# One unit fewer inside the second scan of a complex recurrence followed by a mixture of experts

## The chip, the cores and the metric

The kernel runs on one core of one Trainium2 chip. The metric is the device time of one execution in microseconds (us); the times shown are those of separate executions, and the profile is of one more execution.

## What is computed

A complex diagonal recurrence over 768 steps for 4 batches and 8 heads of 48 channels, and then a mixture of 8 experts (of which each token takes one) on its 3072 output rows. Cut to what matters:

```python
for t in range(S):                                   # S = 768
    new_re = ar * S_re - ai * S_im                   # ar, ai: a_re, a_im with their magnitude capped
    new_im = ar * S_im + ai * S_re
    kv = einsum('bhd,bhe->bhde', k[:, :, t], v[:, :, t])
    S_re, S_im = new_re + kv, new_im
    y[:, :, t] = einsum('bhd,bhde->bhe', q[:, :, t], S_re)
x = y as 3072 rows of 384
expert = argmax(x @ w_gate);  gate = softmax(x @ w_gate)[expert]
out[i] = gate[i] * (relu(x[i] @ w1[expert[i]]) @ w2[expert[i]])
```

## The kernel before

**Attention, in chunks.** The 768 steps are cut into 8 chunks of 96. Within a chunk the recurrence is turned into products: `Att.scan_ops` runs backwards over the 96 steps on VectorE (DVE) and builds the running products of the complex coefficients, 128 rows (batch, head, chunk) at a time. There are two groups of 128 rows, g = 0 for batches 0 and 1 and g = 1 for batches 2 and 3, so there is a first scan and a second scan, each in 7 segments of 8 or 16 steps. One step is a multiplication (L221, `xy`) and an addition (L232, `a`), each dependent on the one before. A step is written in one piece each when some other operation stands behind it in the list, and in two halves each where nothing does (`halves`, L234). `norm_ops` prepares the coefficients of a segment, `post_ops` scales q and k by the products (`qko`) and writes them to the DRAM scratch `scr` from POOL (L296, L299).

**Units.** A unit is one chunk of one batch: unit n is chunk n // 2 of batch n % 2, and units 16 and up are those of the second group. A unit loads its rows from `scr` (`qkc`, stage L, on SP), transposes them on TensorE (PE; `tr`, stages T0 to T3, copied out by ScalarE, ACT), multiplies (`pa`, A0 and A1), masks on DVE (M0 and M1, L366), sums the state (S on PE, `s` L375; D on DVE, L385 and L387; U; ZA, L403; ZB, L408; with `sx`, a copy with its halves swapped, by two DMAs), and makes the output (`y`) and the routing. A chunk that is the last of its batch (units 14 and 15) has no S. The table `SLOT` spreads the stages of a unit over several slots: slot n holds S of unit n, T1, T2, T3 and T0 of unit n + 1, the load L of unit n + 2, and so on. In the names printed below, `s_6` is S or D of chunk 6 (unit 12 at its first occurrence, unit 13 at its second), and `tr_7_0_1` is T1 of chunk 7.

**What sets the order.** Units of the first group need only the first scan, so their slots are laid into the second scan, where DVE is the engine with the chain. `Att.dve_ops` writes that order: it gives slot n a due time `t0 + (n + 2) * dt` against a planned length of the scan segments, and places the stages between the steps. Slots that are not placed in the scan or among the operations behind its last step (the `tail`) come in the loop of `tile_recurrence__then__moe_kernel` (L1319), one after another, with nothing of a scan between them. DVE, PE, ACT and SP follow this written order there, and each engine takes its instructions in order.

**The experts.** `Moe.run` loops over 8 experts and 8 slices of 128 hidden columns: `first` (`ph`, L981), ReLU and its rounding rest (`hh`, `hl`), `second` (`my`, L989). Weights come as `raw` and are split in two parts (`hi` by ACT, `lo` by DVE). The rows of the next expert are loaded from `disp` (`xr`, L910, on SP) and turned on PE (`mt`, L919). In this stage the order on PE, DVE and ACT isn't written by hand: a scheduler that plans with estimated times sets it when the kernel is built. SP's order is written.

The lines that the prediction's steps touch are L221, L232, L366, L375, L403, L408 (scan and units), L346 (load of `qkc`), L296 and L299 (`scr`), L870 (weights), L910 and L919 (rows of the next expert).

Of the kernel before, what the change touches and what calls it, by code (L numbers as in the profile page):

```python
# [36 lines left out]
NORM_AT[NS + 4] = NORM_AT[NS + 4][:6] + (.42, .45) + NORM_AT[NS + 4][8:]  # L37
POST_AT = [(0, .138, .138, 0, .42, .421, .55, .55, .68)] * NS + \
          [(.015, .354, .354, .18, .58, .647, .7, .7, .8)] * NS
POST_AT[NS - 2] = (0, .138, .138, 0, .48, .56, .62, .62, .72)  # L40
POST_AT[NS - 1] = (0, .041, .042, .021, .39, .39, .45, .5, .54)

# [7 lines left out]
SLOT_B = [y for x in SLOT_B for y in ([("W", -3)] if x[0] == "R2" else []) + [x] + ([("P", -3)] if x[0] in ("R3", "U") else [])]  # L50

ALONE = 14
CAP = 0.9990000128746033


# [6 lines left out]
class Att:  # L62
# [387 lines left out]
    def dve_ops(self, slots, t0, dt):  # L450


        sl = [(g, j) for g in range(2) for j in range(NS)]
        norms = [self.norm_ops(*x) for x in sl]
        posts = [self.post_ops(*x) for x in sl]
        ahead = [f for x, f in zip(NORM_AT[1], norms[1][1]) if x < 0]
        out = [norms[0][0], norms[1][0]] + norms[0][1][:5] + ahead[:1] + norms[0][1][5:] + ahead[1:]
        now = None
        self.begin = len(out)
        for k, (g, j) in enumerate(sl):  # L460
            if (g, j) == (1, 0):
                now = 0
                self.half = len(out)
            scan = self.scan_ops(g, j)
            at = [(0.13 if k + 1 < len(sl) else .62, 0, posts[k][0])]
            if k + 2 < len(sl):
                at.append((0.16, 0, norms[k + 2][0]))
            if k + 1 < len(sl):
                at += [(x, c, f) for x, c, f in zip(NORM_AT[k + 1], norms[k + 1][2], norms[k + 1][1]) if x >= 0]
            if k + 2 < len(sl):  # L470
                at += [(1 + x, c, f) for x, c, f in zip(NORM_AT[k + 2], norms[k + 2][2], norms[k + 2][1]) if x < 0]
            if k > 0:
                at += zip(POST_AT[k - 1], posts[k - 1][2], posts[k - 1][1])
            if j == 0 and g:
                at.append((0.56, .8, lambda: (self.pend_copy(0), self.pend_test(0), self.pend_cols(0))))
            length = len(scan) * .25 + sum(c for _, c, _ in at)
            if g:
                unit = []

                while slots and slots[0][0] < ALONE and t0 + (slots[0][0] + 2) * dt < now + length:  # L480
                    n, stage, c = slots.pop(0)
                    unit.append((t0 + (n + 2) * dt - now, c, stage))
                    length += c
                at += [(x / length, c, f) for x, c, f in unit]
                now += length

            spots, cur = [[] for _ in scan], 0
            full = [False] * len(scan)
            for x, c, f in sorted(at, key=lambda t: t[0]):
                p = x * len(scan)  # L490
                cur = min(max(p, cur + 1 if c and full[int(cur)] else cur), len(scan) - .01)
                spots[int(cur)].append(f)
                full[int(cur)] |= c > 0
            for i, (op, fs) in enumerate(zip(scan, spots)):
                m = i - i % 2
                out.append(op[not (full[m] and full[m + 1])])
                out += fs

        tail = posts[-1][1]
        out = out[:len(out) - len(spots[-1])]  # L500
        rest = spots[-1]
        while slots[0][0] < ALONE - 1:
            rest.append(slots.pop(0)[1])
        assert len(rest) == 21
        out += tail[:1] + rest[:7] + tail[1:2] + rest[7:11] + tail[2:4] + rest[11:14] + tail[4:] + rest[14:]
        out += [lambda: self.pend_copy(1), lambda: self.pend_test(1), lambda: self.pend_cols(1)]
        return out

# [756 lines left out]
def kernel(ctx, tc, q, k, v, a_re, a_im, w_gate, w1, w2, out):  # L1265
    nc = tc.nc
    const = ctx.enter_context(tc.tile_pool(name="const", bufs=1))
    dram = ctx.enter_context(tc.tile_pool(name="dram", bufs=1, space=DRAM))
    ident = const.tile([128, 128], F32, name="ident")
    flag = const.tile([1, 1], I32, name="flag")  # L1270
    box = {}
    with ExitStack() as c_main, ExitStack() as c_att:
        cp = c_main.enter_context(tc.tile_pool(name="cp", bufs=1))
        x_pool = c_main.enter_context(tc.tile_pool(name="x_pool", bufs=1))
        att = Att(cp, c_att, tc, dram, ident, q, k, v, a_re, a_im)
        disp = dram.tile([E_ * T, XW], F32, name="disp")
        route = att.route = Route(tc, cp, x_pool, att.ps, ident, disp, w_gate, T, CUTS, LATE)
        with ExitStack() as c_moe:
            with ExitStack() as c_dve:
                att.open_dve(c_dve)  # L1280
                hand = {mybir.EngineType.PE, mybir.EngineType.DVE, mybir.EngineType.Activation, mybir.EngineType.SP}
                slots = att.slots()
                ops = att.dve_ops(slots, 6.5, 10.25)
                with tc.manual_schedule(engines={mybir.EngineType.DVE, mybir.EngineType.Activation}):
                    for op in ops[:att.begin]:
                        op()
                with tc.manual_schedule(engines={mybir.EngineType.DVE}):
                    for op in ops[att.begin:81]:
                        op()
                    route.constants()  # L1290
                    clear = route.clear_ops() + att.clear_ops()
                    for i, op in enumerate(ops[81:att.half], 81):
                        op()
                        if i % 8 == 0 and clear:
                            clear.pop(0)()
                    assert not clear
                with tc.manual_schedule(engines=hand):
                    for op in ops[att.half:]:
                        op()
            att.third(c_att)  # L1300
            moe = Moe(c_moe, tc, ident, disp, w1, w2, out)
            with tc.manual_schedule(engines=hand):
                room = [att.bufs["qkc"][i] for i in range(3)]
                route.room = room[:2]
                route.hook, shift, early, end, gates = moe.turn_ops(att.ps, LATE, route.parts, room[2])
                todo = [(14.5, lambda: nc.vector.memset(room[2][C:], 0.0)), (20, moe.numbers)]
                for p in range(Moe.NP):
                    at = 16 + 3 * p
                    todo += [(at, lambda p=p: part(p))]
                todo.sort(key=lambda x: x[0])  # L1310

                def part(p):
                    loads, splits = moe.weight_ops(0, p)
                    loads[0]()
                    n = 16 + 3 * p
                    todo.extend([(n + 1.5, loads[1]), (n + 2.5, splits[0]), (n + 3, splits[1]), (n + 4, splits[2]), (n + 4.5, splits[3])])
                    todo.sort(key=lambda x: x[0])
                loaded = False
                for i, (n, op, _) in enumerate(slots):  # L1319
                    while todo and todo[0][0] <= n:  # L1320
                        todo.pop(0)[1]()
                    op()
                    if n > 30.8 and not loaded:
                        moe.load()
                        loaded = True
                    if i == len(slots) - 9:
                        for kk in range(KT):
                            shift(kk)
                assert not todo and not route.ready
                for kk in range(KT):  # L1330
                    early(kk)
                for kk in range(KT):
                    end(kk)
                route.rest()
                while route.ready:
                    route.pace()
                route.totals()
                gates()
            route.sort()
            moe.order = route.order  # L1340
            covered = uncovered(nc, cp, att.sums, att.small, route, flag)
            c_att.close()
            moe.open(c_moe)
            moe.run(lambda: covered(moe.ps))
    go = nc.values_load(flag, min_val=0, max_val=1)
    with tc.If(go > 0):
        General(tc, dram, ident, q, k, v, a_re, a_im, w_gate, w1, w2, out)
# [27 lines left out]
```

## Time and profile before

| | us |
|---|---|
| the profiled execution | 671.0, its span 669.3 |
| three further executions | 673.67, 674.87, 2745.45 |
| their median | 674.87 |
| mean granted TensorE clock in the profile | 0.92 of full speed |

An engine's busy time is given for stretches of the span, counted in us from its start. Until about 283 us the two scans run; until about 420 us the units of the second group run; then the experts. A row of a timeline gives the start, the duration, the line, the operation, output and inputs, how many instructions were merged, and in brackets the idle time ahead of it with what ended it. An instruction's duration may overlap the next one's: the step from one start to the next start tells what an instruction costs in a stream. The granted clock is 1.00 at 2.4 GHz and 0.50 at 1.2 GHz.

### The profile page before, as it was taken

The page shows a single profiled execution, that of the slowest core. Times are in us where ns is not written, and L with a number is a line of the kernel's source. Part 1 is how long each engine was busy: PE and PEld are TensorE (multiplying, and loading weights), DVE is VectorE, ACT ScalarE, POOL GpSimd, SP SyncE. Part 2 cuts the span into 40 slices and gives each one's busy share as a digit, 9 for nine tenths or more (in the row PEclk, how much of TensorE's full clock was granted, in tenths as well). Part 3 has the DMA queues.
Part 4 walks back from the last instruction along what each step waited for, and adds up shares of the span by engine and source line. Part 5 has one row for each costly group of instructions (what it writes and reads, how often), then busy time and mean ns, then how long its engine had stood idle before and what let it go on. Part 6 is the DMA issues. An engine that isn't in the chain of part 4 may idle for free.

```text
span 669.3 us, 12570 instructions
## 1 busy us (share of the span) xinstructions
PE 544.7 (81%) x4455; PEld 472.1 (71%) x4455; DVE 479.7 (72%) x1428; ACT 345.4 (52%) x789; POOL 92.8 (14%) x140
## 2 busy tenths in 40 slices
PE   0344434248798999899999999999999999999994
PEld 0122212126587877789999888899999999999993
DVE  5999999999999999827657776465455545564531
ACT  7456534476788886544554553244444443443420
POOL 8030000000000000101322221101120202021111
PEclk9776656676899999989999999999999999999998
DMA  5299444596659777776988742583535362636101
GB/s 189 66 319 324 165 165 138 192 224 201 193 163 252 189 180 223 248 152 160 217 228 226 179 111 70 156 252 92 171 94 176 104 182 92 201 88 200 35 35 35
DMA packets 73239, 111.89 MB, mean 167 GB/s; under 512 B 6402, under 2 KB 63045, under 8 KB 71888
## 3 DMA queue, kind: packets, MB, share of 16 engines
q1 hardware_dynamic: 66384, 77.13, 42.7%
q0 software_dynamic: 6784, 33.88, 15.0%
q8 instruction: 37, 0.61, 0.4%
q14 instruction: 34, 0.28, 0.1%
HBM read 72.99 MB, written 34.26 MB: 160 GB/s over the span
## 4 chain that ended last, share of the span: by engine, by line
PE 60%; DVE 23%; ACT 8%; issue 4%; DMA 4%; POOL 1%; SPq 0%; POOLq 0%; DVEq 0%; ACTq 0%
PE ph L981 15%; PE my L989 14%; DVE xy L221 5%; PE tr L354 4%; PE pa L362 4%; DVE a L232 4%; PE s L375 3%; PE y L418 3%; DVE qko L292 2%; PE x L610 2%; PE y L423 2%; DVE a L202 2%; PE xp L135 2%; PE my L1003 2%; PE wp L135 2%
## 5 line engine op out<-in xcount | busy, mean ns | idle before, releaser
L135 PE MATMUL xp<-a,ident 128*128 128x384 f32 x84 | 48.2, 739 | 90.2 <-ACT a L162 90.2
L880 DVE TENSOR_TENSOR lo<-raw,hi 128x384 fp32r<-128x384 f32 (+2 forms) x128 | 66.5, 553 | 65.5 <-ACT hi L879 55.9
L135 PEld LDWEIGHTS xp<-a,ident 128*128 128x128 f32 x84 | 23.0, 289 | 110.1 <-ACT a L162 78.3
L879 ACT CAST hi<-raw 128x384 fp32r<-128x384 f32 (+2 forms) x128 | 60.0, 512 | 55.1 <-PE ph L981 42.5
L221 DVE TENSOR_TENSOR xy<-a 128x96 f32<-128x96 f32 (+1 forms) x299 | 74.6, 279 | 0.6
L354 PE MATMUL tr<-ident,qkc 96*96 96x96 f32 x512 | 65.6, 252 | 11.0 <-DMA qkc<-scr 6.9
L981 PE MATMUL ph<-xh,hi 128*128 128x448 f32 (+4 forms) x192 | 69.7, 365 | 1.1 <-DVE hl L1027 0.9
L981 PE MATMUL ph<-xl,hi 128*128 128x448 f32 (+4 forms) x192 | 67.8, 353 | 0.0
L981 PE MATMUL ph<-xh,lo 128*128 128x448 f32 (+4 forms) x192 | 67.7, 353 | 0.0
L1027 DVE SCALAR_TENSOR_TENSOR hl<-ph,hh 128x448 fp32r<-128x448 f32 (+4 forms) x64 | 37.4, 586 | 39.0 <-ACT hh L1026 37.9
L1026 ACT ACTIVATE hh<-ph 128x448 fp32r<-128x448 f32 (+4 forms) x64 | 32.8, 514 | 61.0 <-PE ph L981 60.6
L989 PE MATMUL my<-hl,hi 128*128 128x448 f32 (+4 forms) x168 | 60.2, 358 | 0.0
L354 PEld LDWEIGHTS tr<-ident,qkc 96*96 96x96 f32 x512 | 47.6, 129 | 17.5 <-issue 6.7
L989 PE MATMUL my<-hh,lo 128*128 128x448 f32 (+4 forms) x168 | 59.9, 356 | 0.0
L989 PE MATMUL my<-hh,hi 128*128 128x448 f32 (+4 forms) x168 | 56.1, 360 | 0.1
L232 DVE TENSOR_TENSOR a<-xy 128x48 f32<-128x48 f32 (+1 forms) x296 | 55.1, 215 | 0.4
L362 PE MATMUL pa<-qT,kT 128*96 128x96 f32 x512 | 54.8, 251 | 0.0
L362 PEld LDWEIGHTS pa<-qT,kT 128*96 128x96 f32 x512 | 50.6, 168 | 1.4 <-issue 1.0
L954 POOL DMA_INDIRECT out_dram<-o,xr x26 | 28.9, 1111 | 157.7 <-DVE o L953 155.9
L630 POOL DMA_INDIRECT disp<-x,idx x32 | 30.1, 939 | 116.5 <-DVE idx L629 64.7
L418 PE MATMUL y<-a_sb,v 128*64 128x96 f32 x512 | 42.3, 253 | 2.3 <-ACT lt L621 1.7
L375 PE MATMUL s<-v,qkc 128*96 128x96 f32 x448 | 44.1, 253 | 0.0
(196 smaller groups left out, 1187.4 us busy)
## 6 DMA issues: line engine op xcount, KB each, us to landing
raw<-in_moe_w_dram SPq DMA_DIRECT2D x64, 384.0 KB
qkc<-scr SPq DMA_DIRECT2D x32, 528.0 KB
scr<-qko POOLq DMA_DIRECT2D x10, 1536.0 KB, 6.9
disp<-fill POOLq DMA_DIRECT2D x7, 772.0 KB, 17.6
v<-in_v_dram SPq DMA_DIRECT2D x32, 144.0 KB
xr<-disp SPq DMA_DIRECT2D x6, 675.5 KB
sx<-s SPq DMA_DIRECT2D x56, 72.0 KB
a<-in_a_re_dram SPq DMA_DIRECT2D x10, 384.0 KB
```

Of the source, the lines that this page charges most:

```text
L135: nc.tensor.matmul(out=pt[:, :m], lhsT=self.ident, rhs=t[:, h:h + m], start=i == 0, stop=i == 1)
L221: nc.vector.tensor_tensor(out=st['xy'][:, :, cs].rearrange("p (u z) d -> p u z d", u=2), in0=crossed(a4[:, s, 1, cs]), in1=w, op=ALU.mult)
L232: nc.vector.tensor_tensor(out=o, in0=xy[:, 0:4:2, cs], in1=xy[:, 1:4:2, cs], op=ALU.add)
L354: nc.tensor.transpose(out=pt[:, h * C:h * C + C], in_=qk(slice(0, C), 4 * hh + h, slice(z_ * C, z_ * C + C)), identity=self.ident[:C, :C])
L362: nc.tensor.matmul(out=pa[:, h * C:h * C + C], lhsT=kT[:, 4 * hh + h], rhs=qT[:, 4 * hh + h], start=True, stop=True)
L375: nc.tensor.matmul(out=ps[:, h * D:h * D + C], lhsT=qk(slice(None), h, slice(C, 2 * C)), rhs=v[:, h * D:h * D + C], start=True, stop=True)
L418: nc.tensor.matmul(out=py[o:o + DP, i // 2 * C:i // 2 * C + C], lhsT=v[:, h * D:h * D + DP], rhs=a_sb[:, h, :], start=True, stop=c == 0)
L879: nc.scalar.copy(out=hi[i][:, s], in_=raw[i][:, s])
L880: nc.vector.tensor_tensor(out=lo[i][:, s], in0=raw[i][:, s], in1=hi[i][:, s].bitcast(F32), op=ALU.subtract)
L981: nc.tensor.matmul(out=ph[:, :WIDTHS[e]], lhsT=a[:, k, fs], rhs=r[:, k, :WIDTHS[e]], start=k == 0 and i == 0, stop=k == KT - 1 and i == 2)
L989: nc.tensor.matmul(out=py[m][:, :WIDTHS[e]], lhsT=a[:, f % self.PF, ms], rhs=r[:, :WIDTHS[e]], start=f == 0 and i == 0, stop=f == NF - 1 a ...
L1027: nc.vector.scalar_tensor_tensor(out=hl[:, :w], in0=ph[:, :w], scalar=0.0, in1=hh[:, :w].bitcast(F32), op0=ALU.max, op1=ALU.subtract)
```

## The change

One table entry, one limit and one spacing change, and the order of three stages behind the scan.

```diff
+POST_AT[-2] = POST_AT[-2][:8] + (.99,)
 ...
 ALONE = 14
+HELD = 13
 ...
-                while slots and slots[0][0] < ALONE and t0 + (slots[0][0] + 2) * dt < now + length:
+                until = HELD if k + 1 < len(sl) else HELD - 2 + 2 / len(SLOT)
+                while slots and slots[0][0] < until and t0 + (slots[0][0] + 2) * dt < now + length:
 ...
-        while slots[0][0] < ALONE - 1:
+        while slots[0][0] < HELD - 1:
             rest.append(slots.pop(0)[1])
 ...
-        out += tail[:1] + rest[:7] + tail[1:2] + rest[7:11] + tail[2:4] + rest[11:14] + tail[4:] + rest[14:]
+        out += tail[:1] + rest[1:3] + rest[:1] + rest[3:7] + tail[1:2] + rest[7:11] + tail[2:4] + rest[11:14] + tail[4:] + rest[14:]
 ...
-                ops = att.dve_ops(slots, 6.5, 10.25)
+                ops = att.dve_ops(slots, 6.5, 10.75)
```

The slots placed in the scan and its tail end one slot earlier (HELD instead of ALONE), the loop of L1319 starts one slot earlier, and the due times of the slots in the scan lie 10.75 instead of 10.25 planned us apart. The last operation of the last but one segment's `post_ops` (which makes `qko` and writes it to `scr`) gets a later place.

On DVE, from the addition that ends the second scan (`pend`), before:

```order
L232 TENSOR_TENSOR pend_131<-xy_6_0_2743 128x2x48
L366 TENSOR_TENSOR a_sb_111<-pa_5_0_2666,mask 96x384
L292 TENSOR_TENSOR qko_5_2600<-a_1_5_1822,v_1_5_2654 128x16x96
L366 TENSOR_TENSOR a_sb_111<-pa_5_1_2707,mask 96x384
L387 TENSOR_TENSOR s_6_2784<-s_6_2746,z_112 96x384
L403 TENSOR_TENSOR sx_5_2662<-sx_5_2662,pcol_98 96x384
```

and at the same place of the changed kernel:

```order
L234 TENSOR_TENSOR pend_131<-xy_6_0_2654 128x2x48
L368 TENSOR_TENSOR a_sb_110<-pa_5_0_2581,mask 96x384
L294 TENSOR_TENSOR qko_5_2512<-a_1_5_1776,v_1_5_2561 128x16x96
L368 TENSOR_TENSOR a_sb_110<-pa_5_1_2628,mask 96x384
L389 TENSOR_TENSOR s_5_2696<-s_5_2658,z_115 96x384
L405 TENSOR_TENSOR sx_5_2577<-sx_5_2577,pcol_98 96x384
```

The stream of units stands one unit further back against the scan: D of unit 12 (`s_6`) stood behind the scan's last step, now D of unit 11 (`s_5`) does. From the second scan's first step to `pend` DVE has 56 operations of units (L366, L385, L387, L403, L408) before and 51 now, and of its 96 steps 35 are written in halves before and 38 now.

On PE, around the two transposes `pt` that read the end of the second scan, before:

```order
L362 MATMUL pa_6_1_2836<-qT_105,kT_108 96x96 x4
L354 MATMUL tr_6_1_1_2843<-ident,qkc_101 96x96 x4
L375 MATMUL s_6_2890<-v_103,qkc_101 96x96 x8
L324 MATMUL pt_0_2858<-ident,pend_131 96x128
L324 MATMUL pt_1_2861<-ident,pend_131 96x128
L354 MATMUL tr_7_0_1_2902<-ident,qkc_100 96x96 x4
```

and now:

```order
L364 MATMUL pa_5_1_2748<-qT_107,kT_109 96x96 x4
L356 MATMUL tr_6_1_1_2762<-ident,qkc_100 96x96 x4
L377 MATMUL s_6_2809<-v_102,qkc_100 96x96 x8
L326 MATMUL pt_0_2777<-ident,pend_131 96x128
L326 MATMUL pt_1_2780<-ident,pend_131 96x128
L356 MATMUL tr_6_0_1_2821<-ident,qkc_101 96x96 x4
```

S of unit 13 stood ahead of `pt` and T1 of unit 14 behind; now S of unit 12 stands ahead and T1 of unit 13 behind. From here to the start of the experts the rows of PE, DVE and ACT are the same, with one more slot of units to come.

On PE at the head of the experts, where the products of expert 0's second hidden slice (`my0`, `my1`, `my2` from `hh_1`) are followed by those of its fourth (`ph_3`), before:

```order
L989 MATMUL my0_0_5136<-hh_1_5149,hi1_0_0_3122 128x448
L989 MATMUL my1_0_5137<-hh_1_5149,hi1_0_0_3122 128x448
L989 MATMUL my2_0_5138<-hh_1_5149,hi1_0_0_3122 128x448
L981 MATMUL ph_3_5176<-xh_0_2888,hi0_0_1_3487 128x448
L981 MATMUL ph_3_5176<-xl_0_2889,hi0_0_1_3487 128x448
```

and now:

```order
L992 MATMUL my0_0_5142<-hh_1_5155,hi1_0_0_3128 128x448
L992 MATMUL my1_0_5143<-hh_1_5155,hi1_0_0_3128 128x448
L992 MATMUL my2_0_5144<-hh_1_5155,hi1_0_0_3128 128x448
L922 MATMUL mt_1_0_5270<-ident_60,xr_1_5205 128x112 x4
L922 MATMUL mt_1_1_5312<-ident_60,xr_1_5205 128x112
L984 MATMUL ph_3_5182<-xh_0_2807,hi0_0_1_3493 128x448
```

The transposes of expert 1's rows (`mt` from `xr`) now stand ahead of `ph_3`; before, the first of them stood 51 rows further on. On SP, the read of the final flag (L1345) stands two weight loads earlier than before.

## Rows read from the trace of the kernel before

**Rows 1.** The page, chain that ended last, shares by engine

```profile
PE 60%; DVE 23%; ACT 8%; issue 4%; DMA 4%; POOL 1%; SPq 0%; POOLq 0%; DVEq 0%; ACTq 0%
```

**Rows 2.** Busy time by stretch (us and instructions), granted clock, DMA share, GB/s

```profile
143.00:200.00 57.00, 46.01 (x373) 35.16 (x372) 56.25 (x180) 43.77 (x107) 1.09 (x2) 0.85 0.68 192
200.00:268.00 68.00, 63.10 (x750) 52.93 (x749) 64.60 (x168) 54.78 (x151) 1.59 (x3) 1.00 0.80 210
283.00:420.00 137.00, 131.72 (x1753) 120.24 (x1754) 87.38 (x312) 64.69 (x166) 28.22 (x30) 0.99 0.68 166
420.00:660.00 240.00, 238.22 (x1308) 225.83 (x1306) 124.67 (x263) 96.34 (x211) 34.55 (x31) 1.00 0.43 132
```

**Rows 3.** Timeline of DVE near the end of the second scan

```profile
262.61 0.42 DVE L221 TENSOR_TENSOR xy<-a 128x96 f32<-128x96 f32 x2
...
263.18 0.55 DVE L281 TENSOR_TENSOR qko<-wp,v 128x384 f32<-128x384 f32 x1
...
264.68 0.35 DVE L221 TENSOR_TENSOR xy<-a 128x192 f32<-128x192 f32 x1
264.95 0.55 DVE L281 TENSOR_TENSOR qko<-wp,v 128x384 f32<-128x384 f32 x1
265.42 0.25 DVE L232 TENSOR_TENSOR a<-xy 128x96 f32<-128x96 f32 x1
265.58 0.95 DVE L284 SCALAR_TENSOR_TENSOR v<-qko,v 128x768 f32<-128x768 f32 x1
```

**Rows 4.** Waits of DVE, 143 to 268 us: total, times, longest

```profile
DVE sx L403 <- DMA sx<-s: 1.6, 2, 1.2
DVE s L387 <- PE s L375: 0.8, 1, 0.8
DVE lnn L190 <- ACT lnn L179: 0.5, 1, 0.5
```

**Rows 5.** Chain in order of time: S of two units in a row

```profile
326.36 1.36 PE s L375 x16
332.89 1.36 PE s L375 x16
```

**Rows 6.** Timeline of PE around loads of `qkc`

```profile
250.85 0.34 PE L354 MATMUL tr<-ident,qkc 96*96 96x96 f32 x2 [0.59 <-DMA qkc<-scr]
...
274.88 1.52 PE L375 MATMUL s<-v,qkc 128*96 128x96 f32 x16
...
281.86 0.49 PE L354 MATMUL tr<-ident,qkc 96*96 96x96 f32 x4
285.90 0.84 PE L354 MATMUL tr<-ident,qkc 96*96 96x96 f32 x4 [3.54 <-DMA qkc<-scr]
```

**Rows 7.** Timeline of SP (its queue): the two loads that those waited for

```profile
243.76 0.82 SPq L346 DMA_DIRECT2D qkc<-scr  x2
...
276.44 1.79 SPq L346 DMA_DIRECT2D qkc<-scr  x2
```

**Rows 8.** Busy time by stretch, behind the hole, and behind the load of `xr`

```profile
285.90:289.10 3.20, 3.20 (x23) 2.64 (x24) 1.11 (x2) 1.19 (x3) 0.00 (x0) 0.50 0.78 151
...
426.60:430.30 3.70, 3.70 (x20) 3.41 (x19) 0.27 (x1) 0.00 (x0) 0.00 (x0) 1.00 0.72 186
```

**Rows 9.** Timeline of PE at the head of the experts

```profile
427.31 0.37 PE L981 MATMUL ph<-xh,hi 128*128 128x448 f32 x1
...
438.08 0.55 PE L919 MATMUL mt<-ident,xr 112*128 112x112 f32 x4
```

**Rows 10.** Timeline of SP, and the chain there, at the same place

```profile
426.68 0.34 SPq L910 DMA_DIRECT2D xr<-disp  x1
...
427.23 5.20 DMA raw<-in_moe_w_dram
```

**Rows 11.** DMA issues: line, operation, count, KB each

```profile
xr<-disp SPq DMA_DIRECT2D x6, 675.5 KB
raw<-in_moe_w_dram SPq DMA_DIRECT2D x64, 384.0 KB
```

## Prediction

> **What bounds the kernel now.** Start with the chain that ended last: PE holds 60% of it, DVE 23% [rows 1]. The busy time by stretch tells where each counts. From 143 to 268 us, which is the second scan but for its start, DVE is busy for 120.9 of 125 us: the scan is a chain of dependent steps with other work between them, and it is DVE's. PE is nearly as full in the later part (63.1 of 68 us) at a granted clock of 1.00, and slower in the earlier (0.85). From 283 us on PE has no slack: 131.7 of 137 us in the units of the second group, 238.2 of 240 us with the experts [rows 2]. So a microsecond by which the scan ends sooner is a microsecond gained, and every piece of PE work that is moved behind the scan, and every wait of PE there, is paid in full. DMA is busy for 0.80 of its time in the scan [rows 2]; loads of `qkc` are late there at times.
>
> **The change part by part.**
>
> *The slot behind the scan.* One slot of a unit now runs where PE is the bound. S of one unit starts 6.53 us after S of the one before [rows 5]: **+6.53**.
>
> *The hole that it fills in part.* Behind the scan stands a hole of PE. S of unit 13 ends at 276.40, the load of unit 15 can start then and is issued at 276.44, and T1 of unit 15 runs only at 285.90, 3.54 us after PE was ready [rows 6, 7]. That load took 9.46 us to use; one issued at 243.76 took 7.09 (PE waited for it until 250.85) [rows 6, 7]. Now S of unit 12 stands at that place, and it is the load of unit 14 that T1 waits for. Between the two PE has what it had before and, since unit 13 has an S where unit 14 had none, 1.36 us more [rows 5]. With a load that takes as long the hole shrinks from 3.54 to 2.18: **-1.36**. If the load takes 7.09 us it is gone (-3.54). The load of unit 15 comes a slot later, when the writes of `scr` have ended; it has 2.18 plus 5.17 us of work (a slot without S) to land in, 7.35 in all. At 7.09 it is hidden, at 9.46 there is a second hole of 2.1. I take none, since it is issued clear of those writes, and keep 2.1 as an end. The load of unit 16 has one slot more of cover than before.
>
> *The scan with five operations fewer.* DVE loses M0, M1, D, ZA and ZB of one unit between the scan's first step and `pend` (56 to 51 in the order). An operation of 384 columns, as these are, costs 0.47 us from its start to the next (264.95 to 265.42): 2.35 us. Three steps more are written in halves. A halved step costs 0.57 us (262.61 to 263.18), a step in one piece with other work behind each part 0.27 + 0.16 = 0.43 [rows 3]: 3 x 0.14 = 0.42 back. That leaves 1.93. DVE's waits in this stretch are 2.9 us in all: 1.6 for the DMA of `sx`, 0.8 for S on PE, 0.5 for ACT [rows 4]. With wider spacing and 6.5 us less of PE's work in the scan, I let the wait for PE go and keep those for DMA and ACT, whose traffic is the same: 1.93 + 0.8 = **-2.73**. The ends are 4.83 (all waits go) and 0 (new waits on `sx` eat the gain).
>
> *What else moves in the scan.* Norm and post operations of the scan stand some places earlier against the units on PE and ACT; their counts are the same, and DVE's steps, not they, hold the scan (ACT 98.6 of 125 us [rows 2]). The later place of the last `qko` is where it stood already, behind `pend`. Both at nothing; without that cover they are in the end of 0 above.
>
> *The head of the experts.* This the diff doesn't show, the order does. The transposes of expert 1's rows now stand on PE ahead of `ph_3`, the row that started at 427.31; before, they ran at 438.08, long after their rows had landed [rows 9]. SP issues the load of those rows at 426.68, and the first weight load behind it at 427.23 [rows 10]; nothing that leads there is moved by the change, for it hangs on the scatter of the last tokens and on the sorting of the experts. So PE arrives 0.63 us after the issue of a load of 675.5 KB [rows 11], and all its later work waits behind it. When do the rows land? Not shown, but bounded. From 426.60 to 430.30 all DMA moved 186 GB/s x 3.70 us = 688 KB [rows 8], so not before 430.3. The weight load issued behind it had landed by 427.23 + 5.20 = 432.43 [rows 10]; I take that as the late end. The stall is 3.0 to 5.1; I take the middle, 431.4: **+4.1**. No idle time of PE follows that could give it back [rows 2]. The work of the twelve transposes itself is only moved.
>
> The page "DMA: Bandwidth & Descriptors" of the Trainium skill (Anatomy of one DMA) fits a transfer by 2.0 us plus its bytes over 436 KB per us, measured on the software path. By it this load of 675.5 KB would take 3.6 us, the stall would be 3.0 and the sum 1.1 us smaller. The row behind it speaks against the fit here: the 384 KB of weights took 5.20 us [rows 10, 11], where it gives 2.9.
>
> *The clock behind that stall.* After the hole of 3.54 us PE ran at a granted clock of 0.50, which is 1.2 GHz, from 285.9 to 289.1 [rows 6, 8]: 3.2 us in which half the work was done, 1.6 lost. A stall of 4.1 us is nearest to that row: **+1.6**, with nothing as the other end (where it falls against the clock's changes isn't known). For the hole behind the scan, now 2.2 us, I leave the loss as it is; its end is -1.6.
>
> *SP's earlier read of the flag* delays weight loads of expert 2 at most; they are issued ahead of their use by several slices, so nothing. Without cover it would be one load, 5.2 us [rows 10].
>
> **Sum:** 6.53 - 1.36 - 2.73 + 4.1 + 1.6 = +8.1 us. The profiled execution took 671.0 us in its own time (span 669.3 and 1.7 around it); it would take 679.1. The median of the runs shown is 674.87, 3.9 above that execution, so I predict 674.9 + 8.1 = **683.0 us**, 1.2% more. A measurement of this kernel can tell about 2% from no change, which is 13.5 us; the forecast is no measurable change, on the slow side.
>
> **The rivals.**
>
> 1. *The load behind the scan lands in time* (20%). It takes 7.09 us as the one at 243.76 did, the hole closes (another -2.18) and PE keeps its full clock behind it (-1.6): +4.3, 679.2. For it: wider spacing. Against: the same writes of `scr` fall into the same microseconds.
> 2. *No stall at the experts* (10%). The rows land before PE arrives, or PE arrives later for a reason not seen: the sum loses 5.7, +2.4, 677.3. Against: 0.63 us between issue and arrival.
> 3. *The scan doesn't end sooner* (8%): the change doesn't do what it says. The freed 1.93 us turn into waits for `sx` (1.6 us of them already [rows 4]) and the second hole of 2.1 opens: +2.7 + 2.1 = +12.9, 687.8.
> 4. *Slower by more than 2%* (5%): TensorE's clock in the scan. In the earlier part, where PE waits more, it was granted 0.85, in the later part 1.00 [rows 2]. One unit less and wider gaps let PE wait more in the later part too. A stretch at 0.50 as behind the hole costs 1.6 us of PE's work. The verdict turns at 13.5 - 8.1 = 5.4 us, so when more than three such stretches fall where PE holds the units back; with four, +14.5, 689.4. Against: DVE has the chain there, so that the first of them would be hidden.
> 5. *As fast as before or faster* (2%): hole and clock loss gone, all of DVE's waits gone, no stall: 6.53 - 3.54 - 1.6 - 4.83 = -3.4, 671.5.
>
> **How the numbers follow.** The forecast has 55%; its own ends reach from 677 (all of the scan's waits gone) to 687 (late rows, second hole). The range of 676 to 687 also holds rivals 1 and 2; rival 3 lies just above it, 4 and 5 outside, and with the outer parts of the forecast some 2 in 10 are left out. Slower by over 2%, above 688.4: rival 4 and a part of rival 3 and of the forecast's far end, 7%. Faster by over 2%, below 661.4: no case reaches it, 1%. Within: 92%.
>
> **What would show each step.** The slot: PE's `s` rows 6.5 us apart behind `pt`, one more of them than before. The scan: the row of DVE that writes `pend`, 2.7 us earlier if the step is right, unmoved in rival 3. The hole: T1 of unit 14 with an idle time of about 2.2 us ahead of it, none in rival 1, and behind it a clock of 0.50. The experts: the first `mt` from `xr` with an idle time of 3 to 5 us ended by the DMA of `xr`, and a stretch at 0.50 behind it; without that row the largest single term is wrong. Rival 4: a granted clock below 1.00 between 200 and 268 us.

## The result, and the profile after

The changed kernel took 684.34 us (median of four executions, 684.31 to 684.49), the kernel before 674.27 in the same comparison. The ratio is 1.0135, with a 95% interval from 1.0106 to 1.0164: slower, clear of the noise, and within 2%. By the two medians the difference is 10.1 us, by the ratio 9.1; without the execution of 2745.45 us, which is one of the four of the kernel before, that kernel's median is 673.67 and the difference 10.7. The prediction was 683.0 us, with a range from 676 to 687. The total came out almost right, but one of its terms was wrong and two others were mis-sized.

The profiled execution of the changed kernel has a span of 682.8 us, that of before 669.3. In the changed kernel's listing every line stands two or three numbers further down (L366 became L368, L919 became L922). The chain that ended last, shares by engine, against [rows 1]:

```profile
PE 62%; DVE 21%; ACT 6%; DMA 5%; issue 3%; POOL 1%; SPq 0%; POOLq 0%; DVEq 0%; ACTq 0%
```

PE still holds it, a little more than before. The busy time by stretch (us and instructions of PE, PEld, DVE, ACT and POOL, then granted clock, DMA share and GB/s), the later part of the second scan, then about the units of the second group and the experts, against [rows 2]:

```profile
200.00:268.00 68.00, 61.16 (x671) 49.44 (x670) 61.51 (x164) 51.12 (x137) 1.60 (x3) 0.95 0.70 194
288.00:425.60 137.60, 133.90 (x1810) 121.85 (x1809) 88.75 (x314) 66.02 (x172) 28.37 (x30) 1.00 0.70 169
425.60:666.00 240.40, 235.40 (x1279) 223.07 (x1278) 123.76 (x262) 96.91 (x211) 32.67 (x29) 0.99 0.43 131
```

The first row holds the surprise: the granted clock of this stretch was 1.00 before and is 0.95 now, and DVE is busy for 61.5 us where it was for 64.6. The waits of DVE from 143 to 268 us (total, times, longest) say where its time went. They are 5.6 us, against 2.9 in [rows 4]:

```profile
DVE sx L405 <- DMA sx<-s: 2.0, 1, 2.0
DVE s L389 <- PE s L377: 1.8, 2, 1.0
DVE qko L283 <- ACT v L275: 0.9, 1, 0.9
DVE a_sb L368 <- PE pa L364: 0.6, 1, 0.6
DVE lnn L192 <- ACT lnn L181: 0.3, 1, 0.3
```

Two stretches at a clock of 0.50 lie in the scan, each behind a wait of PE, and in each of them the transposes `wp` of a post operation run at half pace. The timeline of PE at the two places (the number in brackets is the idle time ahead and what ended it):

```profile
215.42 0.60 PE L356 MATMUL tr<-ident,qkc 96*96 96x96 f32 x4 [1.64 <-ACT qT L358]
215.82 4.44 PE L137 MATMUL wp<-qko,ident 128*128 128x384 f32 x8
...
241.90 0.51 PE L356 MATMUL tr<-ident,qkc 96*96 96x96 f32 x4 [2.38 <-DMA qkc<-scr]
242.64 4.54 PE L137 MATMUL wp<-qko,ident 128*128 128x384 f32 x8
```

The waits of DVE that follow, in the timeline of DVE of the same execution: two behind the first stretch, for `pa` and for S of a unit, and one behind the second, for `v`.

```profile
222.91 0.55 DVE L368 TENSOR_TENSOR a_sb<-pa,mask 96x384 f32<-96x384 f32 x1 [0.65 <-PE pa L364]
224.60 0.55 DVE L389 TENSOR_TENSOR s<-s,z 96x384 f32<-96x384 f32 x1 [0.97 <-PE s L377]
246.39 0.56 DVE L283 TENSOR_TENSOR qko<-wp,v 128x384 f32<-128x384 f32 x1 [0.93 <-ACT v L275]
```

Behind the scan, the hole of PE against [rows 6], and at the head of the experts the transposes of expert 1's rows against [rows 9], in the timeline of PE:

```profile
286.99 0.51 PE L356 MATMUL tr<-ident,qkc 96*96 96x96 f32 x4 [1.50 <-DMA qkc<-scr]
...
438.46 1.20 PE L922 MATMUL mt<-ident,xr 112*128 112x112 f32 x5 [3.98 <-DMA xr<-disp]
```

The load that the second row waits for, in the timeline of SP, where it was issued 0.76 us before PE was ready for its rows (434.48):

```profile
433.72 0.34 SPq L913 DMA_DIRECT2D xr<-disp  x1
```

in the chain, with the 4.69 us that it took:

```profile
433.72 4.69 DMA xr<-disp
```

and the busy time of the stretch behind the stall, at a granted clock of 0.51:

```profile
437.60:444.50 6.90, 6.04 (x19) 5.48 (x20) 2.71 (x6) 2.72 (x6) 0.00 (x0) 0.51 1.08 352
```

To find where the 13.5 us between the two spans came from, cut both executions at the same four operations: the `qko` of 128x768 elements at about 155 us on DVE (up to which the order of all engines is the same in both), `pend`, S of unit 16, and the first `ph`. The table has this for all kernels of this study, one profiled execution of each; what each is, is told below. A profiled execution is not always near its kernel's median: that of all_before was the longest of its twelve, those of all_after, third_before and third_after the shortest of theirs.

| us | to `qko` | scan, `qko` to `pend` | of it DVE waits | `pend` to S of unit 16 | to first `ph` | experts | span |
|---|---|---|---|---|---|---|---|
| before | 154.07 | 113.52 | 2.9 | 30.06 | 120.95 | 250.7 | 669.3 |
| changed | 155.41 | 114.25 | 5.7 | 33.16 | 122.80 | 257.2 | 682.8 |
| hand_before | 154.75 | 113.89 | 3.6 | 29.74 | 121.22 | 251.0 | 670.6 |
| hand_before_early | 155.29 | 113.81 | 3.5 | 30.03 | 121.45 | 256.7 | 677.3 |
| hand_before_fill | 155.31 | 114.49 | 3.9 | 29.36 | 120.95 | 255.8 | 675.9 |
| hand_after | 155.56 | 113.83 | 5.5 | 33.83 | 121.03 | 253.8 | 678.0 |
| hand_after_1025 | 155.13 | 113.48 | 4.9 | 37.47 | 120.95 | 251.3 | 678.3 |
| all_before | 155.64 | 114.55 | 4.0 | 32.31 | 121.44 | 250.9 | 674.8 |
| all_after | 155.51 | 111.25 | 3.1 | 33.16 | 120.96 | 250.9 | 671.8 |
| all_after_again | 155.47 | 110.94 | 2.8 | 35.33 | 121.01 | 250.9 | 673.6 |
| all_after_1025 | 154.55 | 112.53 | 3.9 | 35.20 | 121.64 | 250.9 | 674.8 |
| all_after_1050 | 154.38 | 111.07 | 3.4 | 33.99 | 121.01 | 250.9 | 671.3 |
| third_before | 154.34 | 113.62 | 3.1 | 28.94 | 120.95 | 251.2 | 669.0 |
| third_after | 155.30 | 110.81 | 2.6 | 32.58 | 120.94 | 250.9 | 670.5 |

Read the first two rows: +1.3 ahead of the change's place, +0.7 in the scan, +3.1 behind it, +1.9 in the units of the second group, +6.5 with the experts. The first of these is no effect of the change: the first column runs from 154.07 to 155.64 with nothing changed there. The fourth stands at 120.9 to 121.6 in every other kernel, those with the same order among them, so the 122.80 is put down to that execution: PE waits there 0.61 us for DVE and 0.73 us for ACT (at 367.9 and 373.8), and in hand_after, which has the same order in this stretch, it does not. The other three were put to experiments.

### The profile page after: what moved, and what is told of

It is laid out like the page before. It is cut to its first block, busy times and chain, and to the rows that moved or that the text cites. A ratio compares the mean times of both kernels' runs of the same rounds, so it can differ in the third digit from the quotient of the medians.

```text
span 682.8 us, 12584 instructions
## 1 busy us (share of the span) xinstructions
PE 552.3 (81%) x4455; PEld 475.7 (70%) x4455; DVE 481.1 (70%) x1434; ACT 346.1 (51%) x789; POOL 93.1 (14%) x140
## 4 chain that ended last, share of the span: by engine, by line
PE 62%; DVE 21%; ACT 6%; DMA 5%; issue 3%; POOL 1%; SPq 0%; POOLq 0%; DVEq 0%; ACTq 0%
PE ph L984 16%; PE my L992 14%; DVE xy L223 5%; PE tr L356 5%; PE pa L364 4%; PE s L377 3%; DVE a L234 3%; PE y L420 3%; PE wp L137 3%; DMA qkc<-scr 3%; PE y L425 2%; PE xp L137 2%; PE x L613 2%; DVE qko L294 2%; PE my L1006 2%
## 5 line engine op out<-in xcount | busy, mean ns | idle before, releaser
L1030 DVE SCALAR_TENSOR_TENSOR hl<-ph,hh 128x448 fp32r<-128x448 f32 (+4 forms) x64 | 37.5, 587 | 39.6 <-ACT hh L1029 38.5
L368 DVE TENSOR_TENSOR a_sb<-pa,mask 96x384 f32<-96x384 f32 x64 | 34.1, 548 | 11.8 <-PE pa L364 11.6
```

Of the source, the lines that this page charges most:

```text
L368: nc.vector.tensor_tensor(out=a_sb[:C, 4 * hh:4 * hh + 4, :], in0=st[hh][:, :4 * C].rearrange("p (h t) -> p h t", h=4), in1=self.mask.unsq ...
L1030: nc.vector.scalar_tensor_tensor(out=hl[:, :w], in0=ph[:, :w], scalar=0.0, in1=hh[:, :w].bitcast(F32), op0=ALU.max, op1=ALU.subtract)
```

## The experiments

### The stall at the head of the experts, put into the kernel before

Theory: PE has no slack with the experts, so the wait for the rows and the half clock behind it are paid in full. First a control, since the order of PE there comes from a scheduler and had to be written by hand:

```diff
-        c_order.enter_context(self.tc.manual_schedule(engines={SP}))
+        c_order.enter_context(self.tc.manual_schedule(engines={SP, PE}))
 ...
             for op in later.pop(s, []):
                 op()
+            if s == 7:
+                c_order.close()
+                c_order.enter_context(self.tc.manual_schedule(engines={SP}))
```

> The kernel before, with the order of PE in the first eight slices of the experts written by hand in the order of the program (the transposes of expert 1's rows behind the slices 3, 4 and 5 as in the code). It is the control for the kernels that differ from it. Both theories: the order is nearly the one that the scheduler chose, the rows have long landed when the transposes come, so no idle time ahead of the first mt and the time of before, 674 us, within 2 us.

Measured: 673.54 us, ratio to before 1.0012 (0.9993 to 1.0031), no idle time at `mt`. The hand order costs nothing that can be told. Now the transposes early, with nothing else different:

```diff
-                    put(s + ((2, 4, 5, 6) if e else (3, 5, 6, 7))[i], op)
+                    put(s + ((2, 4, 5, 6) if e else (2, 2, 2, 5))[i], op)
```

> hand_before with one thing different: the transposes of expert 1's rows stand on PE ahead of ph_3, as in the changed kernel. Theory A (a wait of PE here is paid in full, and the half clock behind it too, since PE has no slack to the end): an idle time of about 4 us ahead of the first mt, ended by the DMA of xr, a granted clock of 0.50 for some 6 us behind it, and a time 5.7 to 7 us above hand_before, 680 to 681. Rival B (something later, a load of weights or the last scatter, sets the end, and PE catches up): the same idle time in the profile, but a time within 2 us of hand_before.

Measured: 679.06 us, ratio 1.0105 (1.0077 to 1.0132), 5.5 us above hand_before. Theory A, at the low end of its 5.7 to 7 us. The timeline of PE:

```profile
433.50 1.26 PE L919 MATMUL mt<-ident,xr 112*128 112x112 f32 x8 [4.08 <-DMA xr<-disp]
```

and the busy time of the two stretches behind it, the clock in the third figure from the end:

```profile
434.10:437.50 3.40, 3.40 (x13) 3.10 (x11) 2.09 (x4) 1.79 (x4) 0.00 (x0) 0.50 1.07 361
437.50:447.00 9.50, 9.50 (x48) 8.70 (x48) 4.49 (x9) 4.29 (x10) 0.00 (x0) 1.00 0.81 241
```

The wait is 4.08 us and the clock is at 0.50 for 3.4 us, half of which is lost: 4.1 + 1.7 = 5.8. The table has 256.7 - 251.0 = 5.7 with the experts. So the two together are the whole price, and nothing is given back. The clock stayed down for half as long as in the changed kernel.

To take the two parts apart, PE was given work during the wait:

```diff
             pt = self.ps.tile([128, 512], F32, tag="tr", ...)
+            if e == 1 and k == 0:
+                for _ in range(24):
+                    nc.tensor.matmul(out=pt[:, :T], lhsT=hi_of_expert_0, rhs=xh_0, start=True, stop=True)
```

> hand_before_early with 24 products of 448 columns ahead of the first transpose of expert 1's rows, whose result is overwritten: PE works through the 4.1 us in which it waited there. It is work added that the reference does not need. At the 0.20 us from one such product to the next they take 4.9 us. Theory A (the stall's price has two parts, the wait itself and the half clock behind it): no stretch at 0.50 behind it (3.4 us in hand_before_early, so 1.7 lost), the wait of 4.1 replaced by 4.9 of work: 679.1 - 1.7 + 0.8 = 678.2. Rival B (the half clock behind the stall costs nothing, or comes all the same): 679.1 + 0.8 = 679.9, with the stretch at 0.50 as before.

Measured: 677.91 us, ratio 1.0082 (1.0050 to 1.0113). With the experts 255.8 us, 0.9 less than hand_before_early, as theory A has it (1.7 of clock back, 0.8 of work more). The times alone can't tell this kernel from hand_before_early (their intervals overlap); the profile does. The busy time there shows no idle time and a clock of 1.00:

```profile
428.00:440.00 12.00, 12.00 (x65) 11.08 (x64) 5.06 (x10) 4.09 (x9) 0.00 (x0) 1.00 0.94 289
```

### The stall taken out of the changed kernel

The same hand order of PE as in hand_before, put into the changed kernel (by the same edit):

> The changed kernel with the hand-written order of PE at the head of the experts that hand_before has: the transposes of expert 1's rows come late again. Theory A (stall of 3.98 us and half clock of 3.0 us belong to the head alone): 684.3 - 7.0 = 677.3 us, 3 us above hand_before. Rival B (the end is set later): 684, 10 us above hand_before, with no idle time ahead of mt. By the prediction's own sum without its two terms at the experts it would be 674.3 + 2.4 = 676.7, with a scan that ends 2.7 us sooner; the trace of the changed kernel shows the scan ending no sooner, so that other waits must have given back as much.

Measured: 680.82 us, ratio 1.0128 (1.0099 to 1.0156), between the two. The stall at `mt` was gone, but of the 6.5 us only 3.4 came back with the experts. Another wait stood there. It is in the timeline of PE:

```profile
443.01 0.47 PE L984 MATMUL ph<-xh,hi 128*128 128x448 f32 x1 [2.58 <-DVE hl L1030]
```

and the timeline of ACT shows why:

```profile
431.29 0.55 ACT L1029 ACTIVATE hh<-ph 128x448 fp32r<-128x448 f32 x1 [2.58 <-PE ph L984]
438.51 0.93 ACT L882 CAST hi<-raw 128x512 fp32r<-128x512 f32 x2 [6.68 <-DMA raw<-in_moe_w_dram]
440.75 0.92 ACT L882 CAST hi<-raw 128x512 fp32r<-128x512 f32 x2 [1.31 <-DMA raw<-in_moe_w_dram]
441.58 0.54 ACT L1029 ACTIVATE hh<-ph 128x448 fp32r<-128x448 f32 x1
```

ACT has the splits of two weight tiles ahead of the ReLU of slice 3, and stands still until those weights land, while the last product of `ph` of that slice had started at 434.56. In hand_before one tile stands ahead of it. ACT's and DVE's order was still the scheduler's, and it had placed them differently too. So both were written by hand (`engines={SP, PE, DVE, Activation}` in the edit above), in both kernels:

> hand_before with the orders of ACT and DVE in the first eight slices of the experts written by hand too, in the order of the program. It is the control for all_after. In hand_after both splits of the second weight tile (hi0_1_1) stood on ACT ahead of the ReLU of slice 3 (hh_3), in hand_before only those of the first; in both all_ kernels none does. All theories: hand_before's time, 673.5 us, or up to 2 us less, since no slice waits behind a split whose weights have not landed.

> The changed kernel with the same hand-written orders at the head of the experts. The spans of hand_after and hand_before differ by 7.4 us: +0.8 ahead of the change's place, -0.1 in the scan, +4.1 between the scan's end and S of unit 16, -0.2 in the second group's units, +2.75 in the experts. Theory A (the 2.75 us are the split ahead of hh_3 alone: ACT waits for weights, the ReLU behind it comes late, PE waits 2.6 us): they go, and all_after is 4 to 5 us above all_before (0.6 to 0.7%), with no idle time over 1.2 us ahead of PE's ph rows. Rival B (the later start of the experts meets late weights in any order): still 7 us above all_before, with a wait of PE for hl or for the weights.

Measured: all_before 673.72 us, ratio 1.0010 (0.9990 to 1.0030); all_after 675.45, ratio 1.0046 (1.0022 to 1.0069). With the experts both take 250.9 us, as before: the 6.5 us of the changed kernel were the scheduler's order and nothing else, and rival B falls. But the change then costs 1.7 us by the medians and 2.4 by the ratios (the two intervals overlap a little), less than the 4 to 5 that theory A expected. The table points to the scan: that of all_after took 111.25 us, 2.6 less than that of hand_after, which has the same order there. How much of it a median execution keeps isn't shown, since the profile of all_after is of its shortest execution, 2.0 us below its median.

### Why the scan ended no sooner, and then did

The first suspicion was the spacing. It was put back, alone, in hand_after (`att.dve_ops(slots, 6.5, 10.25)` in place of 10.75):

> hand_after with the spacing of the units in the scan put back from 10.75 to 10.25 planned us. What it tells: why the scan did not end 2.7 us sooner. Theory A (the wider spacing lets PE idle in the scan, its clock falls to 0.50 in stretches there, and DVE waits for S and for the halves of sx): with 10.25 DVE's waits from 143 to 268 us fall from 5.6 to about 2.9 us, no stretch at 0.50 between 200 and 268 us, pend some 2.7 us earlier, and a time of 674.6, 2.7 below hand_after. Rival C (the spacing has nothing to do with it; the waits come with one unit fewer, or with where single operations happen to stand): waits of 5 to 6 us and a time within 1 us of hand_after.

Measured: 677.11 us, ratio 1.0066 (1.0042 to 1.0090), 3.7 us below hand_after. Neither theory holds. Of the 3.7 us the profiles have 2.5 with the experts (251.3 against 253.8): the scheduler put one weight tile ahead of the ReLU of slice 3 here and not two, though nothing was edited there. In the scan the clock stayed at 1.00 from 200 to 268 us, as A wants, but the waits were 4.9 us and the scan took 113.48. The waits had another face. The timeline of PE near the scan's end:

```profile
261.25 2.85 PE L137 MATMUL wp<-qko,ident 128*128 128x384 f32 x8 [1.40 <-ACT qko L259]
```

and that of DVE behind it:

```profile
264.02 0.56 DVE L283 TENSOR_TENSOR qko<-wp,v 128x384 f32<-128x384 f32 x1 [1.83 <-ACT v L275]
```

With the units close together, a post operation's input (`qko` from ACT) comes late to PE, and DVE waits for what follows from it (`v`). Behind the scan, too, PE then waits for `qko` (3.97 us at 269.3, and as long in all_after_1025 below), and S of unit 16 came 37.5 us behind `pend`. In hand_after the `qko` step that waited was the one at 246 us, behind a `wp` of 5.24 us at half clock, and it waited 2.16 us. The timeline of PE at its two waits:

```profile
215.47 0.54 PE L356 MATMUL tr<-ident,qkc 96*96 96x96 f32 x4 [1.64 <-ACT qT L358]
215.84 2.77 PE L137 MATMUL wp<-qko,ident 128*128 128x384 f32 x8
...
240.72 0.85 PE L356 MATMUL tr<-ident,qkc 96*96 96x96 f32 x4 [2.65 <-DMA qkc<-scr]
241.98 5.24 PE L137 MATMUL wp<-qko,ident 128*128 128x384 f32 x8
```

At the first place the clock stayed at 1.00, and DVE had none of the waits for `pa` and S that the changed kernel shows behind it. all_after had no such wait at either place. Its waits of DVE, 143 to 270 us:

```profile
DVE sx L405 <- DMA sx<-s: 2.0, 1, 2.0
DVE s L389 <- PE s L377: 0.8, 1, 0.8
DVE lnn L192 <- ACT lnn L181: 0.6, 2, 0.3
```

and its busy time from 200 to 268:

```profile
200.00:268.00 68.00, 60.84 (x704) 50.29 (x703) 64.14 (x171) 54.39 (x147) 1.59 (x3) 1.00 0.73 198
```

Its PE waited at the same places (1.65 us at 215.4, and here the wait for `qkc`), but its clock stayed at 1.00 and `wp` took 2.85 us:

```profile
240.23 0.51 PE L356 MATMUL tr<-ident,qkc 96*96 96x96 f32 x4 [2.00 <-DMA qkc<-scr]
240.97 2.85 PE L137 MATMUL wp<-qko,ident 128*128 128x384 f32 x8
```

So a new theory: the longer waits of PE that come with the wide spacing let its clock fall in some executions and not in others, and only where it falls is the scan's gain eaten. It was tested with the same kernel once more:

> all_after once more, for a second profile and more times. In the changed kernel's scan PE waits 1.6 us at 215.4 (for ACT) and 2.0 to 2.7 us at 240 to 242 (for a load of qkc); the longest wait of PE there in the kernel before is 1.1. Where the granted clock fell to 0.50 behind those waits (the changed kernel, hand_after), the scan from the qko of 128x768 to pend took 113.8 to 114.3 us with 5.5 to 5.7 of DVE's waits, and where it stayed at 1.00 (all_after) 111.25 with 3.1. Theory D (the clock in the scan decides whether the scan's gain is kept): this profile shows one or the other pair, never a full clock with 113.8 or a fallen one with 111.2, and the executions are spread over some 7 us again, slower where the mean clock is lower. Rival E (the scan was shorter in all_after by the chance of its loads): the pair can be mixed.

Measured: 676.27 us, ratio 1.0056 (1.0035 to 1.0077). The profile: clock 1.00 from 200 to 268 us, scan 110.94, waits 2.8, which is D's second pair. third_after below, with the same order in the scan, makes it three such profiles (110.81 and 2.6), against two with a fallen clock (114.25 and 5.7, 113.83 and 5.5); none is mixed. The same shows place by place. PE waits at both places in all five profiles, ten times in all; the clock fell at three of the ten, and DVE then waited 1.6, 0.9 and 2.6 us behind it, and at the seven where it stayed DVE had no such wait. The spans of the 24 executions of all_after and all_after_again run from 671.8 us at a mean clock of 0.930 to 678.6 at 0.912 (correlation -0.88 and -0.81); those of before go with the clock less closely (-0.5). That clock is the mean of a whole execution, not of the scan. For the scan itself this rests on five profiles, the three without a fall being of short executions, so how often the clock falls is not shown; and why the clock falls behind a wait of 1.64 and 2.38 us in one execution and not behind 1.65 and 2.44 in another is open.

The spacing again, now without the scheduler at the head:

> all_after with the spacing put back from 10.75 to 10.25. Of hand_after_1025 the profile showed no fallen clock from 200 to 268 us, waits of PE of up to 1.4 us there, and yet a scan of 113.5 us with DVE waiting 2.3 us for v (ACT) near its end. Theory D1 (the spacing trades one thing for the other: narrow, no fallen clock, but the post operations' transposes stand late behind the units and DVE waits for v; wide, the wait is gone, but the clock may fall): 677 us, 1 to 2 above all_after, in a narrower spread, a scan of 113.5. Rival D2 (spacing does not matter): all_after's time within 0.7 us, a scan of 111.3 in a profile with a full clock.

> all_after with a spacing of 10.5, half way. Theory D1: a time and a scan between those of 10.25 and 10.75, or like one of them, according to where the transposes wp of the last post operations fall against the units: 675.5 to 677. Rival D2: 675.5, no difference among the three.

Measured: 676.48 us at 10.25, ratio 1.0056 (1.0035 to 1.0078), and 674.55 at 10.5, ratio 1.0021 (1.0003 to 1.0038). The first has the waits for `v` that D1 named, 2.4 us, and a narrower spread (spans 673.9 to 677.6), but its scan of 112.53 us lies between D1's 113.5 and D2's 111.3, and its median is that of 10.75 within 1.0 us, so that the trade is even. At 10.5 the longest wait of PE in the scan was 1.55 us, the waits for `v` 1.3, the scan 111.07. The time at 10.5 is the lowest of the three, below what either theory gave, but its interval overlaps those at 10.75, and it is still not below before. The later place of the last but one segment's last post operation and the new order of the three stages behind the scan stayed in all of them; neither was tried alone.

### The hole behind the scan

The hole was put down to the load of unit 15, which waits for S of unit 13. The third buffer of `qkc` is free from the scan's end on:

```diff
-            return bufs[n % 2 if n < 16 else (n - 14) % 3][i]
+            return bufs[n % 2 if n < 15 else (17 - n) % 3][i]
```

> hand_before with unit 15's rows loaded into the third buffer of qkc, which is free once the scan has ended, and units 16 and up taking the three buffers in the other direction. The load of unit 15 then waits for the scan's operations on DVE and ACT and no longer for S of unit 13. Theory A (the hole behind the scan is that load's lateness: issued when S of unit 13 ends, 9.5 us to use): it is issued some 2 us sooner, right behind the load of v, ahead of the last writes of scr; the hole of 3.1 us shrinks by at least those 2 us, perhaps to none, and with it the half clock: 673.5 - 2 to - 4.8 = 669 to 671.5. Rival B (the load is held by the writes of scr that share the queues, whenever it is issued): it lands at the same time, hole and time unchanged, 673.5; if the loads of units 16 and 17 then come late, above it.

Measured: 671.99 us, ratio 0.9996 (0.9976 to 1.0016). The load was issued at 275.09, 7.1 us behind `pend` (before: 276.44 in [rows 7], 8.9 behind `pend` at 267.59). The timeline of PE:

```profile
284.97 0.26 PE L354 MATMUL tr<-ident,qkc 96*96 96x96 f32 x1 [2.24 <-DMA qkc<-scr]
```

It took 9.9 us to use, where that of before took 9.5, so an issue 1.7 us sooner made the hole 0.9 to 1.3 us smaller. Both theories hold a part. Half clock behind it as before, and no difference in time that can be told. In the changed kernel:

> all_after with the third buffer for unit 15's rows, as in third_before. all_after's profile has two holes behind the scan, 0.39 us for the load of unit 14 and 1.38 for that of unit 15, issued when S of unit 13 has ended. Theory A (the second hole is that load's place): it is issued some 2.5 us sooner, the second hole goes, the first stays, 675.5 - 1.4 = 674. Rival B (the writes of scr hold the loads, so that one issued earlier is late all the same): 675.5, hole as before. In neither case would it be below the kernel before by more than the comparison can tell.

Measured: 675.11 us, ratio 1.0034 (1.0012 to 1.0055). The load of unit 15 was issued 2.1 us sooner behind `pend` and the second hole is gone; the first was 1.26 (0.39 in all_after), `pend` to S of unit 16 is 32.6. By the profile theory A; the times can't tell it from all_after. No kernel of the study beats the one before.

## Why the prediction was right, and where not

*The slot and the hole.* +6.53 for the slot was right: from T1 of unit 13 to the end of its S PE worked 6.7 us (278.77 to 285.49). S of units 12 and 13 stand 7.94 us apart, not 6.5, since the two `pt` and a wait of 0.55 for ACT lie between. The load of unit 14 took 9.40 us to use, as forecast (issued at 277.59), but PE had 0.6 us more ahead of it, so the hole shrank to 1.50 us where 2.18 was forecast, and in the other profiles at this spacing to between 0.39 and 1.26. The half clock behind it, which the prediction left as it was, went with it: from 284 to 290 us the granted clock is 1.00 in the changed kernel. So the term was mis-sized: 6.53 - 2.04 - 1.6 = 2.9, against 3.1 in the table, where the prediction had 5.2. The second hole, an end of the range, came in all_after and all_after_again (1.4 and 1.3 us), not in the changed kernel's profile.

*The scan.* This step failed. It was to end 2.73 us sooner and took 0.73 us longer. The step had two parts. The work was right: the scan less DVE's waits is 113.52 - 2.88 = 110.6 us before and 114.25 - 5.68 = 108.6 now, in the hand-ordered pair 110.3 and 108.4, so 1.9 to 2.1 less where 1.93 was worked out. The waits were wrong, in sign: +2.8 instead of -0.8. The prediction let the wait for S on PE go because PE had less to do; a wait of 0.8 us for S stands in every profile at this spacing all the same. What came on top is what its rival 4 described: PE waits longer, and its clock falls. That rival was set aside with the words that DVE has the chain there, so that the first such stretch would be hidden. It isn't. DVE's chain takes in results of PE: behind the first stretch it waited 1.6 us for `pa` and S of a unit, behind the second 0.9 for a post operation that passes through PE and ACT (`wp`, then `v`). That is 2.55 us, and all_after's waits are those of the changed kernel without these. In profiles where the clock stayed, the scan was 2.3 to 2.7 us shorter than before. That meets the forecast of 2.73 in part by luck: the work was about 2.5 less there than before, not 1.93, and the waits, 2.6 to 3.1 us, had not shrunk by 0.8. So the scan that did not end sooner is rival 3's (without its second hole) and the mechanism is rival 4's, with two stretches where that rival needs four to decide the verdict.

*The experts.* The term that the diff does not show was right: 3.98 us of stall for 4.1, in the changed kernel and (4.08) where it was put into the kernel before. By the fit on the page "DMA: Bandwidth & Descriptors" of the Trainium skill (Anatomy of one DMA), which was measured for DMAs issued from GpSimd, a load of this size takes an estimated 3.6 us, from 2.0 us and 436 KB per us. The trace does not bear that out for this load, which SP issued: it took 4.69 us, and the stall by the fit would have been 3.0 in the prediction's sum.

*The clock behind the stall.* This term was mis-sized: 1.6 forecast, about 3.0 in the changed kernel (6.0 us of work at 0.50), 1.7 in hand_before_early. Taking a single row as its measure was too narrow; the loss should have had 3 us as its other end, not nothing alone.

*Balance.* By the profiles 13.5 us: +1.3 and +1.9 of the executions themselves, +0.7 instead of -2.7 in the scan, +3.1 instead of +5.2 behind it, +6.5 instead of +5.7 with the experts. The misses of the change have both signs (+3.4, -2.1, +0.8) and leave +2.1, and 3.2 us more are of the two executions; against this the prediction started from a median 3.9 us above the profile of before. So that the total came within 1.3 us of the median is in good part luck. The prediction also called its 1.2% no measurable change; the interval of this comparison is 0.3% to either side, and the change shows clear of it. Its ends of 677 and 687 are wider than the cases named beside them: with all of the scan's waits gone its sum gives 680.9, with late rows and a second hole 686.1. Of the ten microseconds 6.5 are the order that a scheduler made at the head of the experts. With all orders there written by hand the change costs two to three (1.0046 and 1.0056 against 1.0010). What is left, one or two, these runs don't place; the scan, 3.0 to 3.4 us longer in the profile of the changed kernel than in theirs at this spacing, is likely, but not shown.

## What to carry to other kernels

Where a scheduler sets a part of the order when the kernel is built, an edit far away can move it, so compare the orders of every engine for the whole program, and price a transfer's consumer that has moved ahead of its landing: here that was over half of the change's cost. The edit can be as small as a spacing in another stage, as hand_after_1025 shows. Taking work out of a chain shortens its work by what it says, but whether the end comes sooner hangs on the waits, so follow each result that the chain takes from the other engines, and ask what a longer idle time does to their pace. A term that rests on a clock wants both outcomes as its ends.

## What the hardware showed that was not expected

Behind waits of PE of nearly the same length the granted clock fell in one execution and stayed in another: 1.64 and 2.38 us with two stretches at 0.50 in the changed kernel, 1.65 and 2.44 us with none in third_after, and in hand_after none behind 1.64 us and one at 2.65. In those stretches `wp`, 2.85 us at 1.00, took 4.4 to 5.2. At stalls of 3.98 and 4.08 us the clock was at 0.50 for 6.8 us (6.0 of them behind the stall's end) and for 3.4 us. A load of `qkc` issued 1.7 us sooner landed less than that sooner (9.9 us to use, against 9.5).
